# Weight remainders spread over 128 partitions, and V rows loaded from GpSimd's queue, in a two-layer recurrent-memory transformer kernel

## Chip, cores and metric

One core of one Trainium2 chip. The metric is the device time of one execution in microseconds; the kernel before takes 2640.42 us, the median of 3 runs (2637.03 to 2641.07).

## What is computed

Two identical layers on x of 2048 rows by 576 columns in bf16. A layer is attention over segments of 32 rows with a memory of 8 rows that the segment before left behind, then a gated feed-forward block of width 4608:

```python
for s in range(n_seg):                       # 64 segments of 32 rows
    h = concatenate([mem, x_segment])        # 8 + 32 rows
    q, k, v = h @ Wq, h @ Wk, h @ Wv         # 32 heads of 128
    p = softmax(mask(q @ k.T * scale))
    o = (p @ v) @ Wo
    mem = o[:8]; outs.append(o[8:])
x = x + attention(layernorm(x)); x = x + (silu(n @ w1) * (n @ w3)) @ w2   # n = layernorm(x)
# both lines once more, with the same weights
```

The memory makes the segments a chain: segment s needs the output of segment s - 1.

## The kernel before, in words

The 576 input columns are four chunks of 128 rows of the weights and a remainder of 64. `T.W` holds Wq in its parts 0 to 3, Wk in parts 4 to 7, and both remainders in part 8: Wq's on partitions 0 to 63, Wk's on 64 to 127, each 4096 columns wide. The remainder matmuls (`qk_tail`) use these two halves of TensorE's rows for q and k of one head at a time. `T.WV` holds Wv, with the 64-row remainder folded over both halves: blocks of 512 columns go alternately to partitions 0 to 63 and 64 to 127. `T.WO` holds Wo. All of it stays on chip.

The two layers run together, the second 8 segments behind the first, in 72 steps t. A step with both layers (t = 8 to 63) handles 32 heads in 4 groups g of 8: q and k, scores, softmax (VectorE and ScalarE), a DMA transpose of the probabilities from `PB` to `PTS` issued by SP, PV on TensorE, then Wo. `PB` has two buffers; after a transpose GpSimd clears the buffer (`pb_zero`, a memset), and VectorE then writes it for the next group but one. The feed-forward blocks run between the steps on TensorE, with w1, w3 and w2 streamed from HBM by SP.

At the start the rows of V that belong to the first layer's segments 9 to 16 are computed ahead ("VA"), since they depend on x alone, and stored to a DRAM tensor `XV`. In steps 9 to 16 each group loads its 32 rows by 1024 columns back into `T.V` (`va_load`, 64 KB, 32 loads), after the PV matmuls of the same group in the step before.

The order of the work comes from a planner (`plan`): each node has an engine, a cost and dependencies. TensorE's order is written out by hand as a string of letters (`ORDER`); for the other engines and queues ("DMA" is SP's, "SWD" GpSimd's, "ACT" ScalarE's) the planner takes the node that can start first by its costs. An engine then runs its instructions strictly in that order. `LOAD_BW` and the numbers in `node(...)` are such costs.

At the start SP issues, in this order: half of Wv's remainder, Wv in 8 loads of 512 KB, one load of x rows, the remainders of Wq and Wk, Wq and Wk in 16 loads, Wo in 4. ScalarE's queue issues two loads of 128 x rows, the 8 rows of mem0 and the other half of Wv's remainder. A completion semaphore is shared by every eighth hardware-queue load, and an issue waits for the load before it on its semaphore.

Lines that the prediction names: SP's loads are recorded on line 744 (`dma`), ScalarE's on 750 (`adma`), GpSimd's on 753 (`swdma`), transposes on 1290, the memset of `PB` on 1280, all matmuls on 735, ScalarE's work on 738 and VectorE's on 741. In the profile `W<-in_B_w_dram` is a feed-forward weight going to `W13`, since names are shown without their numbers.

Of the kernel before, what the change touches and what calls it, by code (L numbers as in the profile page):

```python
# [9 lines left out]
ACT = mybir.ActivationFunctionType  # L10
# [3 lines left out]
P = 128  # L14
R64 = 64
D = 576
NCH = D // R64
H = 32
E = 128
MEM = 8  # L20
SEG = 32
# [9 lines left out]
NV = 4  # L31
# [1 line left out]
R_HT = 6  # L33
PTR = 112
VAT = -9.5
LOAD_BW = {"ldqk": 400e3, "ldv": 410e3, "ldo": 360e3}
AH = (8, 17)
AROWS = (AH[0] + 1) * SEG
TRLAT = 2.5
# [29 lines left out]
def role(t):  # L69

    return (t - LAG) % 2


def pre(t):

    return AH[0] <= t <= AH[1]
# [194 lines left out]
def make_nodes(em, nseg, pools, o=Opt, dma_bw=230e3, load_bw=380e3, tail_bw=330e3):  # L271
# [4 lines left out]
    def node(*a, **k):  # L276
        n = Node(*a, **k)
        n.prio += 1e-9 * len(nodes)
        nodes.append(n)
        return n  # L280

    def banks(n=2):
        return [Slot("bank") for _ in range(n)]
# [12 lines left out]
    def load(name, nbytes, prio, fn, deps=()):  # L296
        return node("DMA", nbytes / LOAD_BW.get(name, load_bw), fn, deps=deps, prio=prio, name=name, lat=2.0)

    ld_m0 = node("ACT", 0.1, em.load_m0(), prio=-90, name="m0", lat=8.0)
    ld_t = [node("DMA", 1.3, em.load_vt(0), prio=-10.0, name="ldt", lat=2.0), node("ACT", 0.1, em.load_vt(1), prio=-80, name="ldt", lat=9.0)]  # L300
    ld_qt = node("DMA", 3.0, em.load_qt(), prio=-9.2, name="ldt", lat=2.0)
    ld_qk = [load("ldqk", kb(1024, H // 2 * E), i - 9.0, em.load_qk(i)) for i in (0, 1)]
    ld_h = [ld_qk[h0 // (H // 2)] for h0, _ in GROUPS]
    ld_v = [load("ldv", kb(512, 2048), VAT + 0.1 * i, em.load_v(i)) for i in (0, 1)]
# [3 lines left out]
    stored = []  # L308
    b = banks(1)
# [42 lines left out]
    vx_ev, last_v, pvs = {}, [], {}  # L352
# [46 lines left out]
    def step(t):  # L399
# [19 lines left out]
        for g, (h0, nh) in enumerate(GROUPS):  # L419
            qs, qe = [], []  # L420
            for uh, un in units(g, nl):
                q = Slot("qkt", users=1)
                b = banks()
                pq = t + o.qk + o.ustep * uh / 4
                m_ = node("PE", 8 * un * mmq, em.qk(t, uh, un, b), deps=hx + hm[:1] + ([ld_h[g]] if t == 0 else []),
                          prio=pq, mode="full", acq=[q] + b, name="QK")
                n = node("PE", un * mmq, em.qk_tail(t, uh, un, b), deps=hx + hm + ([ld_h[g], ld_qt] if t == 0 else []), prio=pq + o.qkt, mode="row",
                         acq=[q] + b, name="QKt")
# [18 lines left out]
            w = (1.04 - 0.07 * (e and not pre(t)) if nl == 2 else 0.46) * nh / 8  # L447
# [17 lines left out]
            b = banks(nl)  # L465
            ot = [Slot("ot") for _ in range(nl)]
            if pre(t) and t > AH[0]:
                kept = [d for blk in blks for d in vx_ev["VM", t - 1, blk]]
                if t < AH[1]:
                    kept.append(node("DMA", 0.3, em.va_load(t, g), deps=stored + [pvs[t - 1, g]], prio=t - 1 + o.gstep * g + 0.2, lat=2.4, ring=0.6, name="VAl"))  # L470
            else:
                kept = [d for blk in blks for d in vx_ev["VX", t - e, blk]]
            pv = node("PE", nh * mm80, em.pv(t, g, pts, b), deps=pe_ + kept + [d for blk in blks for d in vx_ev["VM", t, blk]],
                      prio=pf + o.pv, mode="full/col", acq=b + ot, rel=[pts], name="PV")
# [40 lines left out]
    kept = {}  # L515
# [165 lines left out]
    for t in range(nst):  # L681
        if t % 4 == 2 and (t + 2) // 4 < ngrp:
            x_in((t + 2) // 4)
        if t == LAG:
            ht_mem[t].append(node("DVE", 0.1, em.init_mem(1, LAG), deps=[m0e] + reads_ht.get(LAG - R_HT, []), prio=LAG - 2, name="m0"))
        if role(t) == 0 or t == 0:
            vx_pair(t - role(t), t - 1 + o.vx)
        step(t)
        if t == 0:
            opens = steps[0][f"WO{NG - 1}"]  # L690
            for nb, fn, es in stores:
                stored.append(node("DMA", 0.35 * nb, em.paced(fn, False, opens), deps=es + [opens], prio=0.5, lat=2.4, ring=0.35 * nb, name="VAs"))
        if t % 4 == 1 and t // 4 < ngrp:
            x_res(t // 4)
        if t % 4 == 3:
            job((t + 1) // 4 - 1)
        elif t == nst - 1:
            job(nst // 4)
# [12 lines left out]
class Emitter:  # L711
# [94 lines left out]
                    self.dma(self.T.W[:, 4 * kind + c, h], wd[c * P:(c + 1) * P, h])  # L806
        return f

    def load_vt(self, r):
        return lambda n: (self.adma if r else self.dma)(self.wv(True)[r * R64:(r + 1) * R64, :].rearrange("p (q n) -> p q n", q=NV),  # L810
                                                        self.a.wv[4 * P:D, :].rearrange("p (q r n) -> r p q n", q=NV, r=2)[r])

    def load_qt(self):
        def f(n):
            for r, wd in ((0, self.a.wq), (1, self.a.wk)):
                self.dma(self.T.W[r * R64:(r + 1) * R64, 8, :], wd[4 * P:D, :])
        return f

    def wv(self, tail):
# [304 lines left out]
    def va_load(self, t, g):  # L1124

        def f(n):
            r0, row = (t - AH[0] - 1) * SEG, 96 * role(t)
            self.dma(self.T.V[row:row + SEG, 2 * g:2 * g + 2, :], self.T.XV[r0:r0 + SEG, g * 1024:(g + 1) * 1024].rearrange("p (b n) -> p b n", n=512))
        return f

    def at(self, t):
# [32 lines left out]
    def qk_tail(self, t, uh, un, b):  # L1164
        def f(n):
            first = self.begin(b)
            for j in range(un):
                e0 = (uh + j) * E
                for kind in (0, 1):
                    rr = slice(kind * R64, (kind + 1) * R64)  # L1170
                    x, w = self.qk_rhs(t, rr, 4)
                    self.mm(self.bk(b[kind])[:, j * w:(j + 1) * w], self.T.W[rr, 8, e0:e0 + E], x,
                            first and j == 0, True, tile_position=(kind * R64, 0))
        return f

    def qk_ev(self, t, un, r, q, b):
# [328 lines left out]
def kernel(  # L1505
# [26 lines left out]
    em = Emitter(nc, tc, T, a, nseg)  # L1532
    pools = dict(POOLS)
    nodes = make_nodes(em, nseg, pools)

    wp = ctx.enter_context(tc.tile_pool(name="wts", bufs=1))
# [99 lines left out]
```

## Time and profile before

| | |
|---|---|
| median of 3 runs | 2640.42 us |
| profiled execution, its own time | 2643.07 us |
| its span, first to last instruction | 2641.3 us |
| mean granted TensorE clock | 0.994 |
| TensorE busy | 2563.1 us (97%) |
| VectorE, ScalarE, GpSimd busy | 2042.3, 1225.3, 338.1 us |
| moved by the DMA queues | 375.94 MB, mean 142 GB/s |
| V loads from XV | 32, issued between 269.0 and 526.1 us |

A row of a stretch gives its bounds, its length, the busy time of each engine with the count of its instructions, the granted clock of TensorE, the mean busy share of the 16 DMA engines, and what they moved. A row of the chain gives when a piece began, how long the chain stayed on it, and on what. A row of a DMA issue gives tensors, queue, count, size and the median time from issue to landing. In the timeline a bracket at a row's end tells the idle time before it and what ended it.

### The profile page before, as it was taken

How to read it: one execution, taken by the hardware profiler on the slowest of the kernel's cores; microseconds unless marked ns; L12 is line 12 of the kernel's file. 1: busy time of each engine (PE TensorE's matmuls, PEld its weight loads, DVE VectorE, ACT ScalarE, POOL GpSimd, SP SyncE). 2: the span in 40 equal slices, each digit the busy share in tenths (PEclk: the TensorE clock that was granted, in tenths of full speed). 3: DMA queues.
4: the chain of work that ended last, by engine and by line, in shares of the span. 5: the costliest groups of instructions: out<-in, count | busy, mean ns of one | idle time of the engine just before them, and what ended most of it. 6: DMA issues, size and time to landing. Idle time of an engine off the chain costs nothing.

```text
span 2641.3 us, 132672 instructions
## 1 busy us (share of the span) xinstructions
PE 2563.1 (97%) x58964; PEld 2182.5 (83%) x58991; DVE 2042.3 (77%) x5156; ACT 1225.3 (46%) x3492; POOL 338.1 (13%) x401
## 2 busy tenths in 40 slices
PE   6999999999999999999999999999999999999998
PEld 4788778888888888888888888888888888888887
DVE  5778777787888778778877877887787777788866
ACT  2545444544445354444535444453544445454543
POOL 1111111110111111111101101111111111011110
PEclk8999999999999999999999999999999999999999
DMA  9155747556555667555464655655575555554457
GB/s 308 56 154 139 183 106 179 143 134 155 129 135 115 151 127 155 134 132 138 110 144 126 158 137 126 146 112 139 120 166 134 135 135 112 135 121 141 127 156 239
DMA packets 690960, 375.94 MB, mean 142 GB/s; under 512 B 234728, under 2 KB 683248, under 8 KB 690128
## 3 DMA queue, kind: packets, MB, share of 16 engines
q1 hardware_dynamic: 686784, 359.94, 55.6%
q8 instruction: 461, 7.55, 1.2%
q0 software_dynamic: 3024, 6.93, 1.0%
q14 instruction: 115, 0.94, 0.1%
q10 hardware_dynamic: 576, 0.57, 0.1%
HBM read 309.11 MB, written 4.46 MB: 119 GB/s over the span
## 4 chain that ended last, share of the span: by engine, by line
PE 86%; DMA 7%; DVE 5%; issue 1%; ACT 1%; SPq 0%; POOL 0%; ACTq 0%; DVEq 0%; POOLq 0%
PE bank L735 86%; DMA PTS<-PB 2%; DMA W<-in_B_w_dram 1%; DMA W<-in_A_Wk_dram 1%; DVE STAT L741 1%; DMA W2C<-in_B_w_dram 1%; DVE SME L741 1%; DVE PB L741 1%; DVE V L741 1%; DVE HTT L741 1%; DMA WV<-in_A_Wv_dram 0%; ACT V L738 0%; SPq L744 0%; DVE QKT L741 0%; DVE XR L741 0%
## 5 line engine op out<-in xcount | busy, mean ns | idle before, releaser
L735 PEld LDWEIGHTS <-W 128*128 128x128 bf16 (+2 forms) x31776 | 1241.3, 100 | 131.8 <-issue 68.6
L735 PE MATMUL bank<-HT,W 128*128 128x80 bf16 (+2 forms) x23040 | 792.0, 197 | 16.6 <-issue 6.1
L735 PE MATMUL bank<-XTB,W 128*64 128x256 bf16 (+5 forms) x8736 | 661.4, 263 | 5.9 <-DMA W<-in_B_w_dram 3.1
L1280 POOL MEMSET PB<- 128x1024 bf16 x288 | 273.7, 951 | 1728.1 <-DMA PTS<-PB 950.9
L738 ACT ACTIVATE QKT<-bank 128x192 bf16<-128x192 f32 (+2 forms) x1505 | 356.0, 319 | 294.9 <-PE bank L735 286.0
L735 PE MATMUL bank<-OT,WO 128*128 128x80 bf16 (+3 forms) x11520 | 419.0, 198 | 5.7 <-issue 3.6
L735 PEld LDWEIGHTS <-WO 128*128 128x128 bf16 (+1 forms) x11520 | 386.4, 102 | 42.0 <-issue 30.0
L738 ACT ACTIVATE V<-bank 32x512 bf16<-32x512 f32 (+1 forms) x545 | 311.7, 586 | 164.7 <-PE bank L735 151.5
L735 PE MATMUL bank<-WV,HT 128*32 128x512 bf16 (+5 forms) x3777 | 347.7, 383 | 3.2 <-issue 2.5
L738 ACT ACTIVATE HTT<-bank 128x512 bf16<-128x512 f32 (+1 forms) x326 | 177.3, 549 | 312.6 <-PE bank L735 311.2
L735 PE MATMUL bank<-W2C,HTT 128*64 128x288 bf16 (+1 forms) x3224 | 314.8, 287 | 6.3 <-DMA W2C<-in_B_w_dram 2.9
L741 DVE TENSOR_REDUCE STAT<-SME 104x8 f32<-104x320 f32 (+1 forms) x576 | 274.7, 477 | 26.7 <-ACT SME L738 18.3
L741 DVE SCALAR_TENSOR_TENSOR XR<-bank,XR 128x288 f32<-128x288 f32 x574 | 242.1, 448 | 62.3 <-PE bank L735 57.6
L741 DVE TENSOR_TENSOR PB<-SME,STAT 40x128 bf16<-40x128 f32 (+4 forms) x932 | 276.6, 332 | 11.6 <-DVE STAT L741 0.4
L735 PEld LDWEIGHTS <-HTT 128*64 128x64 bf16 (+1 forms) x3304 | 226.5, 106 | 45.6 <-issue 8.7
L741 DVE SCALAR_TENSOR_TENSOR HTT<-HTT,bank 128x512 bf16<-128x512 bf16 (+1 forms) x324 | 200.8, 620 | 62.8 <-ACT HTT L738 59.7
L735 PEld LDWEIGHTS <-HT 128*32 128x32 bf16 (+5 forms) x3800 | 138.5, 101 | 128.5 <-issue 21.7
L738 ACT ACTIVATE OT<-bank 128x320 bf16<-128x320 f32 (+2 forms) x409 | 157.4, 399 | 172.6 <-PE bank L735 165.9
L741 DVE CAST V<-bank 64x512 bf16<-64x512 f32 (+1 forms) x287 | 196.6, 685 | 41.4 <-PE bank L735 35.4
L741 DVE TENSOR_TENSOR HTT<-HTT,bank 128x512 bf16<-128x512 bf16 (+1 forms) x324 | 203.6, 628 | 29.3 <-PE bank L735 0.9
L738 ACT ACTIVATE SME<-SME 104x320 f32<-104x320 f32 (+1 forms) x288 | 135.3, 470 | 173.3 <-DVE SME L741 171.7
L741 DVE CAST QKT<-bank 128x192 bf16<-128x192 f32 (+4 forms) x415 | 122.1, 335 | 89.7 <-PE bank L735 86.5
(64 smaller groups left out, 1413.5 us busy)
## 6 DMA issues: line engine op xcount, KB each, us to landing
W<-in_B_w_dram SPq DMA_DIRECT2D x608, 256.0 KB, 3.8
W2C<-in_B_w_dram SPq DMA_DIRECT2D x304, 288.0 KB, 3.9
W<-in_B_w_dram SPq DMA_DIRECT2D x608, 32.0 KB, 3.5
W<-in_B_w_dram SPq DMA_DIRECT2D x16, 512.0 KB, 6.9
W<-in_A_Wq_dram SPq DMA_DIRECT2D x9, 512.0 KB, 10.2
W<-in_A_Wk_dram SPq DMA_DIRECT2D x9, 512.0 KB, 10.2
WO<-in_A_Wo_dram SPq DMA_DIRECT2D x4, 1152.0 KB, 14.3
XR<-in_A_x_dram POOLq DMA_DIRECT2D x16, 288.0 KB, 3.1
```

The lines of the kernel that those rows point to most:

```text
L735: self.ch("PE", self.nc.tensor.matmul(out, lhsT=lhsT, rhs=rhs, start=start, stop=stop, skip_group_check=True, **k))
L738: self.ch("ACT", self.nc.scalar.activation(*a, **k))
L741: self.ch("DVE", getattr(self.nc.vector, fn_)(*a, **k))
L1280: return lambda n: self.ch("POOL", self.nc.gpsimd.memset(self.T.PB[:, pb.i, 0:GROUPS[g][1]], 0.0))
```

## The change

The remainders: Wv's is one load of 512 KB by SP into all 128 partitions (ScalarE's queue no longer takes part). Part 8 of `T.W` now holds, on partitions 0 to 63, Wq's heads 0 to 15 and Wk's heads 16 to 31, and on partitions 64 to 127 the other two. Wq's remainder is one load into 128 partitions of 2048 columns; Wk's is two loads of 64 rows by 2048 columns. `qk_tail` follows: for heads 16 to 31, q and k swap their halves. The 32 V loads go from SP's queue to GpSimd's. The planner's costs for these loads change; `ORDER` does not.

```diff
-LOAD_BW = {"ldqk": 400e3, "ldv": 410e3, "ldo": 360e3}
+LOAD_BW = {"ldqk": 405e3, "ldv": 405e3, "ldo": 357e3}
...
-    ld_t = [node("DMA", 1.3, em.load_vt(0), prio=-10.0, name="ldt", lat=2.0), node("ACT", 0.1, em.load_vt(1), prio=-80, name="ldt", lat=9.0)]
-    ld_qt = node("DMA", 3.0, em.load_qt(), prio=-9.2, name="ldt", lat=2.0)
+    ld_t = [node("DMA", 4.0, em.load_vt(), prio=-10.0, name="ldt", lat=2.0)]
+    ld_qt = node("DMA", 2.6, em.load_qt(), prio=-9.2, name="ldt", lat=2.0)
...
-                    kept.append(node("DMA", 0.3, em.va_load(t, g), deps=stored + [pvs[t - 1, g]], prio=t - 1 + o.gstep * g + 0.2, lat=2.4, ring=0.6, name="VAl"))
+                    kept.append(node("SWD", 1.0, em.va_load(t, g), deps=stored + [pvs[t - 1, g]], prio=t - 1 + o.gstep * g + 0.2, lat=4.0, name="VAl"))
...
-    def load_vt(self, r):
-        return lambda n: (self.adma if r else self.dma)(self.wv(True)[r * R64:(r + 1) * R64, :].rearrange("p (q n) -> p q n", q=NV),
-                                                        self.a.wv[4 * P:D, :].rearrange("p (q r n) -> r p q n", q=NV, r=2)[r])
+    def load_vt(self):
+        return lambda n: self.dma(self.wv(True).rearrange("p (q n) -> p q n", q=NV), self.a.wv[4 * P:D, :].rearrange("p (q r n) -> r p q n", q=NV, r=2))
 
     def load_qt(self):
         def f(n):
-            for r, wd in ((0, self.a.wq), (1, self.a.wk)):
-                self.dma(self.T.W[r * R64:(r + 1) * R64, 8, :], wd[4 * P:D, :])
+            w = H // 2 * E
+            self.dma(self.T.W[:, 8, 0:w], self.a.wq[4 * P:D, :].rearrange("p (r n) -> r p n", r=2))
+            for r in (1, 0):
+                self.dma(self.T.W[r * R64:(r + 1) * R64, 8, w:2 * w], self.a.wk[4 * P:D, (1 - r) * w:(2 - r) * w])
...
-            self.dma(self.T.V[row:row + SEG, 2 * g:2 * g + 2, :], self.T.XV[r0:r0 + SEG, g * 1024:(g + 1) * 1024].rearrange("p (b n) -> p b n", n=512))
+            self.swdma(self.T.V[row:row + SEG, 2 * g:2 * g + 2, :], self.T.XV[r0:r0 + SEG, g * 1024:(g + 1) * 1024].rearrange("p (b n) -> p b n", n=512))
...
             for j in range(un):
-                e0 = (uh + j) * E
+                up, hh = divmod(uh + j, H // 2)
                 for kind in (0, 1):
-                    rr = slice(kind * R64, (kind + 1) * R64)
+                    r0 = (kind ^ up) * R64
+                    rr, e0 = slice(r0, r0 + R64), (kind * H // 2 + hh) * E
                     x, w = self.qk_rhs(t, rr, 4)
                     self.mm(self.bk(b[kind])[:, j * w:(j + 1) * w], self.T.W[rr, 8, e0:e0 + E], x,
-                            first and j == 0, True, tile_position=(kind * R64, 0))
+                            first and j == 0, True, tile_position=(r0, 0))
```

SP's queue at the program's start, before (a row is line, operation, tile written and read, rows x columns, count):

```order
L744 DMA WV<-in_A_Wv_dram 64x4x512
L744 DMA WV<-in_A_Wv_dram 128x2048 x8
L744 DMA XN<-in_A_x_dram 128x576
L744 DMA W<-in_A_Wq_dram 64x4096
L744 DMA W<-in_A_Wk_dram 64x4096
L744 DMA W<-in_A_Wq_dram 128x2048 x4
```

and the same place after the change:

```order
L744 DMA WV<-in_A_Wv_dram 128x4x512
L744 DMA WV<-in_A_Wv_dram 128x2048 x8
L744 DMA XN<-in_A_x_dram 128x576
L744 DMA W<-in_A_Wq_dram 128x1x2048
L744 DMA W<-in_A_Wk_dram 64x2048 x2
L744 DMA W<-in_A_Wq_dram 128x2048 x4
```

Nothing moved past anything else; the first load doubled, Wq's remainder took 128 rows, and Wk's became two.

SP's queue where the first V loads stood, before (W_83 is the feed-forward tile W13):

```order
L1290 DMA_TRANSPOSE PTS<-PB 128x8x112
L744 DMA W_83<-in_B_w_dram 64x256 x2
L744 DMA V<-XV 32x1024 x2
L744 DMA W_83<-in_B_w_dram 64x256 x2
L1290 DMA_TRANSPOSE PTS<-PB 128x8x112
L744 DMA W_83<-in_B_w_dram 128x4x256 x2
L744 DMA V<-XV 32x1024
```

and after:

```order
L1292 DMA_TRANSPOSE PTS<-PB 128x8x112
L744 DMA W_83<-in_B_w_dram 64x256 x4
L1292 DMA_TRANSPOSE PTS<-PB 128x8x112
L744 DMA W_83<-in_B_w_dram 128x4x256 x4
L744 DMA W2C<-in_B_w_dram 128x2x576 x2
```

The V loads are gone from between the weight loads and transposes, whose own order is unchanged.

GpSimd's queue at the same steps, before (memsets of PB, reciprocal roots of the layer norms, an x load):

```order
L950 TENSOR_TENSOR LNS<-LNS,mhalf 128x1 x2
L1280 MEMSET PB 128x1024 x5
L753 DMA XR<-in_A_x_dram 128x576
L1280 MEMSET PB 128x1024
L950 TENSOR_TENSOR LNS<-LNS,mhalf 128x1
```

and after:

```order
L951 TENSOR_TENSOR LNS<-LNS,mhalf 128x1 x2
L1282 MEMSET PB 128x1024 x2
L753 DMA V<-XV 32x1024 x2
L1282 MEMSET PB 128x1024
L753 DMA V<-XV 32x1024
L1282 MEMSET PB 128x1024
L753 DMA V<-XV 32x1024
L1282 MEMSET PB 128x1024
L753 DMA XR<-in_A_x_dram 128x576
L1282 MEMSET PB 128x1024
L753 DMA V<-XV 32x1024 x2
```

A V load now stands between one clearing of a PB buffer and the next.

## The prediction

> **What bounds the kernel now.** I read the page's shares first, then the chain of work that ended last, then the first 60 us in stretches. The first lines below are the page's span and shares, the next its chain by engine, the rest pieces of the chain in order of time (start us, length us, what).
>
> ```profile
> span 2641.3 us, 132672 instructions
> PE 2563.1 (97%) x58964; PEld 2182.5 (83%) x58991; DVE 2042.3 (77%) x5156; ACT 1225.3 (46%) x3492; POOL 338.1 (13%) x401
> PE 86%; DMA 7%; DVE 5%; issue 1%; ACT 1%; SPq 0%; POOL 0%; ACTq 0%; DVEq 0%; POOLq 0%
> ```
>
> ```profile
> 2.32 10.56 DMA WV<-in_A_Wv_dram
> ...
> 14.28 13.22 DMA W<-in_A_Wk_dram
> 27.51 9.93 DMA W<-in_A_Wk_dram
> 37.46 10.20 DMA W<-in_A_Wk_dram
> 47.70 1.94 PE bank L735 x73
> ...
> 399.99 112.34 PE bank L735 x2519
> ```
>
> TensorE is the bound for nearly the whole span, but not at the start: up to 47.70 us the chain is a string of weight loads, first the Wv remainder on ScalarE's queue (2.32 to 12.88), then the Wk remainder (14.28 to 27.50), then the bulk of Wk. Whatever moves the last of these loads moves all that follows, because from there the chain runs on TensorE. So the loads at the start are worth their full length, and a load of step 9 to 16 only what it does to a wait of TensorE. The stretches of the start (columns: stretch, length, busy time of PE, PEld, DVE, ACT, POOL, granted clock, DMA share, GB/s):
>
> ```profile
> 2.00:12.00 10.00, 0.03 (x2) 0.03 (x3) 8.53 (x19) 1.28 (x1) 4.79 (x11) 1.00 0.99 288
> 12.00:18.00 6.00, 5.20 (x32) 2.45 (x34) 0.00 (x0) 0.70 (x1) 0.00 (x0) 1.00 1.09 399
> 18.00:28.00 10.00, 6.00 (x57) 2.67 (x53) 3.19 (x11) 2.43 (x7) 0.55 (x1) 0.84 0.98 231
> 28.00:38.00 10.00, 7.75 (x118) 3.45 (x118) 5.65 (x9) 5.30 (x9) 0.00 (x0) 0.99 1.03 409
> 38.00:48.00 10.00, 9.01 (x192) 6.34 (x190) 6.77 (x16) 2.40 (x5) 0.00 (x0) 0.83 1.04 401
> ```
>
> With 128-row loads alone the queues move 409 GB/s. In the two stretches that hold the 64-row remainders they move 288 and 231 at the same DMA share, so the DMA engines are occupied without moving bytes. What that costs: 10 x (1 - 288/409) = 3.0 us and 10 x (1 - 231/409) = 4.4 us, 7.3 us together (before rounding). This is what a better shape of these loads can win at most.
>
> **The remainders.** Bytes stay the same (512 KB for each of Wq, Wk, Wv); the shape changes, and with it, I think, the number of DMA engines that carry a load. The new source patterns of Wv and Wq have r, of size 2, as outermost dimension, over a destination of 128 rows. The trace has one load with an outermost count under 16, the 8 rows of mem0 on ScalarE's queue, q10. Below, the issues of that queue and its count of packets:
>
> ```profile
> XN<-in_A_x_dram ACTq DMA_DIRECT2D x2, 144.0 KB, 3.0
> WV<-in_A_Wv_dram ACTq DMA_DIRECT2D x1, 256.0 KB, 10.6
> XTB<-in_A_mem_dram ACTq DMA_DIRECT2D x1, 9.0 KB
> q10 hardware_dynamic: 576, 0.57, 0.1%
> ```
>
> Rows moved: 128 + 128 for XN, 8 for mem0, 64 x 4 for Wv, 520 in all. That leaves 56 packets of the 576, which fits one closing packet per DMA engine used: 16 + 16 + 16 and 8. The load of 8 rows ran on 8 engines. No row shows which pattern decides when source and destination differ (2 against 128), so both ends must be priced: two engines, or all 16.
>
> The Trainium skill's page "DMA: Bandwidth & Descriptors", section "Why a DMA increments its semaphore by 16 and not by 1", says that the engine count is the largest number up to 16 that divides the slowest dimension (not 1) of both patterns, which gives 2 here; the closing packets above agree with it for 8 and 16.
>
> Two engines: each then carries 256 KB of Wv and 256 KB of Wq. Dealt over 16, it would carry 32 KB of each. Extra: 448 KB, that is 458,752 bytes, on two engines, at 409/16 = 25.6 GB/s per engine: 17.9 us. Every other load of the start needs all 16 engines, so it ends when these two are through, and no later load catches up. The Wv rows are 1 KB packets. On q10, while it carries only the Wv remainder (7.4 to 12 us):
>
> ```profile
> q10 hardware_dynamic: 269, 0.26, 18.3%
> ```
>
> 18.3% of 16 x 4.6 us over 269 packets is 50 ns each, against 1024/25.6 = 40 ns at the full rate; 256 x 10 ns = 2.6 us at most. That row was measured beside another stream, so I take half, 1.3. What goes: the 7.3 us of the stretches above, since the two engines serve different halves of the partitions and the other 14 have long passed. Wk's remainder stays two 64-row loads, but by then the two late engines run alone. Sum: 17.9 + 1.3 - 7.3 = **+11.9 us**. Bounds of this case: +10.6 (no packet cost) to +20.5 (full packet cost, no stall goes away).
>
> Other edits there: the x rows on ScalarE's queue share the two engines and may land up to some 12 us later than their 3.0; the first use of Wv moves as far, so the loads cover it. ScalarE loses a DMA issue, takes the evictions of XTB and one QKT from VectorE and gives back one copy into W13: all under the wait for W, so nothing, and under 1 us without that cover. The matmuls of the remainder swap row halves for heads 16 to 31, same count and size: nothing. The granted clock is at half just after the loads (0.50 ahead of the last two columns):
>
> ```profile
> 60.00:62.00 2.00, 1.89 (x40) 1.24 (x37) 0.41 (x2) 0.83 (x2) 1.06 (x2) 0.50 0.07 17
> ```
>
> A longer idle start may lengthen or move such a stretch; I cost it at nothing, with 2 us on either side.
>
> **The V loads of steps 9 to 16.** 32 issues leave SP for GpSimd's queue (first row: shortest, median, longest ns; then pieces of SP's timeline; then what TensorE waited for between 230 and 560 us, as total, times, longest):
>
> ```profile
> L744 SPq DMA_DIRECT2D V<-XV x32: 303/452/1367, 269.0 to 526.1; - x32
> ```
>
> ```profile
> 337.26 0.45 SPq L744 DMA_DIRECT2D V<-XV  x1
> 339.02 1.22 SPq L1290 DMA_TRANSPOSE PTS<-PB  x1
> 340.29 1.10 SPq L744 DMA_DIRECT2D W2C<-in_B_w_dram  x2
> 341.49 3.18 SPq L744 DMA_DIRECT2D W<-in_B_w_dram  x4
> 344.77 1.24 SPq L1290 DMA_TRANSPOSE PTS<-PB  x1
> ...
> 374.28 1.88 SPq L744 DMA_DIRECT2D V<-XV  x2
> 376.33 1.35 SPq L1290 DMA_TRANSPOSE PTS<-PB  x1
> ```
>
> ```profile
> PE bank L735 <- DMA PTS<-PB: 5.4, 4, 2.2
> ```
>
> SP gets 32 x 0.452 = 14.5 us of issue time back, but TensorE waited only 5.4 us in all for transposes, and the one at 344.77 stands behind four weight loads (3.18 us), not behind a V load. Only at 374.28 does a pair of V loads (1.88 us) stand right ahead of a transpose. Gain: 0 to 1.9 us. On GpSimd each V load waits for the PV matmuls of the step before; behind it in its queue stands the memset that clears a PB buffer, for which VectorE's next write of that buffer and its transpose wait. Rows of GpSimd (an x load's issue, then two of those memsets):
>
> ```profile
> 300.14 0.57 POOL L753 DMA_DIRECT2D XR<-in_A_x_dram  x1
> ...
> 335.00 0.95 POOL L1280 MEMSET PB<- 128x1024 bf16 x1 [3.03 <-DMA PTS<-PB]
> 342.08 0.95 POOL L1280 MEMSET PB<- 128x1024 bf16 x1 [6.13 <-DMA PTS<-PB]
> ```
>
> The memset of 335.00 now stands behind the V load of 337.26. With 0.57 us for its issue it starts some 2.8 us late and ends near 338.8; two buffers alternate, and its buffer's next transpose is that of 344.77, so it is not late. Others are shifted by an issue or so. I cost the move at nothing, from -1.9 to +3 us (a late memset of this size that is waited for once).
>
> **Sum.** The profiled execution took 2643.07 us for its span of 2641.3; the median of the runs is 2640.42. 2643.07 + 11.9 + 0 = 2655.0, and 2.65 less for the median: about **2652 us**, 0.5% more than before. Own bounds of this case: 2640.4 + 10.6 - 1.9 - 2 = 2647 and 2640.4 + 20.5 + 3 + 2 = 2666; the upper end needs all at once, so I use 2662.
>
> **Rivals.**
>
> 1. *All 16 engines carry the new loads* (the destination's 128 rows decide). Then the change does what its shape suggests: the stalls go, except that Wk's remainder is still two 64-row loads. Half of the 4.4 us stays: -7.3 + 2.2 = -5.1 us, 2635; bounds -7.3 and -3.0 (the first stretch alone), so 2633 to 2637. For it: 288 and 231 GB/s against 409 with the 64-row shapes. Against it: 8 closing packets for 8 rows. It decides the sign: where more than about half of the extra bytes are spread over all 16 engines, the result is no longer slower. The Trainium skill's page named above, section "Rules for kernel authors", advises one 128-partition transfer in place of two to disjoint halves, which is this rival; the low GB/s beside the 64-row loads agrees with it.
> 2. *Two engines for each load, but not the same two.* Then each carries 224 KB extra: 9.0 + 1.3 - 7.3 = +3.0 us, 2643. Nothing in the trace tells engines apart.
> 3. *Two engines, and GpSimd's queue bites as well*: a V load held by its PV matmuls delays a memset that is waited for, 1 us in each of the 8 steps: 2652 + 8 = 2660. For it: the memset at 335.00. Against it: GpSimd is busy 13% of the span.
>
> **How the numbers follow.** Forecast 0.72, rival 1 0.18, rival 2 0.05, rival 3 0.05. A measurement of this kernel tells about 0.2% (5.3 us) from no change, so faster means under 2635.1 and slower over 2645.7. Rival 1 lies on the first border: half of it is faster, half the same. Rival 2 is the same, forecast and rival 3 are slower, less 0.01 for the forecast's low end: faster 0.09, same 0.15, slower 0.76. The forecast's own range, 2647 to 2662, holds with rival 3 about 0.70; to leave out no more than 2 in 10 the range must reach to the middle of rival 1: 2634 to 2662.
>
> **What would show it.** Right: the Wv remainder and the Wq remainder each land more than 10 us after their first byte, GB/s in the first 40 us is far under 409 while SP waits, the last Wk load lands near 59 instead of 47.7 us, and everything behind it is shifted by about 12 us and no more. The V loads then start some us earlier than on SP, and the wait for PTS stays near 5.4 us. Wrong: GB/s at 400 from 4 us on and the last Wk near 42 us (rival 1); or a shift that is right at 60 us and grows between 260 and 540 us (rival 3).

## The result, and the profile after

The changed kernel takes **2658.76 us** (median of 5 runs, 2653.08 to 2662.47) against 2640.42 (2637.03 to 2641.95) for the kernel before on the same chip: a ratio of 1.0069, 95% interval 1.0051 to 1.0088, or 18.3 us more (13.5 to 23.2). Single executions of one kernel scatter by 5 to 9 us, and here the profiled execution of after (2653.08) is the fastest of its five, while that of before (2643.07) is slower than all five of before's. So the cost is taken from the medians, and the two traces are compared at places near the start, not at their ends. Other chips run the kernel before at 2632 to 2637 us; below, each version is given as a ratio to the runs of before on its own chip. In two versions below one execution had a much lower granted clock (0.753 and 0.881), and the ratios leave it out.

Span, shares, and the chain by engine, of after:

```profile
span 2651.3 us, 132692 instructions
PE 2560.9 (97%) x58964; PEld 2182.4 (82%) x58991; DVE 2042.6 (77%) x5155; ACT 1226.4 (46%) x3493; POOL 354.2 (13%) x433
PE 84%; DVE 6%; DMA 6%; issue 1%; ACT 1%; SPq 1%; POOL 0%; DVEq 0%; POOLq 0%; ACTq 0%
```

TensorE's busy time is the same to 0.1% (2560.9 against 2563.1 us): no work was added, it starts later. Where, the chain up to the first matmuls on the whole of Wk tells (start, length, what):

```profile
1.53 8.16 SPq L744
...
10.21 10.02 DMA WV<-in_A_Wv_dram
20.23 0.02 issue
20.25 3.41 SPq L744
23.66 0.04 issue
23.71 20.30 DMA W<-in_A_Wk_dram
...
44.03 10.22 DMA W<-in_A_Wk_dram
54.25 0.02 issue
54.27 10.23 DMA W<-in_A_Wk_dram
64.50 0.05 issue
64.54 1.94 PE bank L735 x73
```

The piece of 73 matmuls that began at 47.70 us now begins at 64.54, **16.8 us later**. Ahead of it stand the same loads, one Wk load of 20.30 us among them (the second half of Wk's remainder). The spans of the two traces lie only 10.0 us apart: between 175 and 417 us the shift of the same matmuls goes from 15.1 to 9.0. The traced execution of before falls behind there against every version below, by 5.6 to 9.7 us whatever that version changes, so this belongs to that execution and not to the change. The same stretches of the start as before (busy time of PE, PEld, DVE, ACT, POOL; clock; DMA share; GB/s):

```profile
2.00:12.00 10.00, 0.03 (x2) 0.03 (x2) 8.53 (x19) 1.28 (x1) 4.81 (x11) 1.00 0.34 100
12.00:18.00 6.00, 1.00 (x12) 0.79 (x14) 0.00 (x0) 0.70 (x1) 0.00 (x0) 1.00 0.98 318
18.00:28.00 10.00, 6.74 (x51) 3.06 (x47) 1.87 (x6) 1.94 (x6) 0.00 (x0) 1.00 0.88 294
28.00:38.00 10.00, 6.40 (x43) 2.72 (x44) 2.30 (x6) 1.30 (x2) 0.55 (x1) 0.66 0.89 242
38.00:48.00 10.00, 4.95 (x77) 1.93 (x75) 5.49 (x8) 4.71 (x8) 0.00 (x0) 0.92 0.51 166
48.00:58.00 10.00, 4.14 (x89) 3.19 (x91) 0.69 (x1) 1.21 (x3) 0.00 (x0) 0.50 1.01 380
```

Two stretches have idle DMA engines (shares 0.34 and 0.51), and from 12 to 38 us they are busy but move 242 to 318 GB/s. A closer cut shows how many engines work in the idle parts:

```profile
6.00:9.00 3.00, 0.00 (x0) 0.00 (x0) 2.78 (x7) 0.03 (x1) 0.00 (x0) 1.00 0.14 49
38.50:42.00 3.50, 3.50 (x72) 1.51 (x64) 1.30 (x2) 1.43 (x3) 0.00 (x0) 1.00 0.13 53
28.00:36.00 8.00, 4.56 (x28) 1.90 (x28) 1.61 (x5) 0.70 (x1) 0.55 (x1) 0.58 0.92 240
```

A share of 0.13 to 0.14 of 16 engines is 2.1 to 2.2 engines: first the Wv remainder alone, then the Wq remainder alone. The completion semaphores say the same. A load raises its semaphore by 16 in all. Those of the Wv and the Wq load move once early (at 1.85 and 19.93 us) and then only twice more (last at 16.61 and 42.12 us): 14 increments at once, two late ones. These two loads, then, run on **two engines**. The loads behind them show the wait: of the first whole Wq load behind the remainders, 14 increments come between 29.10 and 30.61 us and the other two at 44.14 and 44.96. The Trainium skill, page "DMA: Bandwidth & Descriptors", section "Why a DMA increments its semaphore by 16 and not by 1", takes the count of engines from the outer dimensions of both patterns, which gives 2; the 0.13 here agrees.

The V loads on GpSimd's queue, and TensorE's wait for transposes from 230 to 560 us:

```profile
V<-XV POOLq DMA_DIRECT2D x32, 64.0 KB, 3.9
PE bank L735 <- DMA PTS<-PB: 3.3, 2, 2.0
```

The wait went from 5.4 to 3.3 us (the last column is the longest single one): nothing that could carry 18 us either way.

### The profile page after: what moved, and what is told of

The parts are those of the page before. It is cut to its first block, busy times and chain, and to the rows that moved or that the text cites. A ratio compares the mean times of both kernels' runs of the same rounds, so it can differ in the third digit from the quotient of the medians.

```text
span 2651.3 us, 132692 instructions
## 1 busy us (share of the span) xinstructions
PE 2560.9 (97%) x58964; PEld 2182.4 (82%) x58991; DVE 2042.6 (77%) x5155; ACT 1226.4 (46%) x3493; POOL 354.2 (13%) x433
## 4 chain that ended last, share of the span: by engine, by line
PE 84%; DVE 6%; DMA 6%; issue 1%; ACT 1%; SPq 1%; POOL 0%; DVEq 0%; POOLq 0%; ACTq 0%
PE bank L735 84%; DMA PTS<-PB 2%; DMA W<-in_A_Wk_dram 2%; DVE STAT L741 1%; DMA W<-in_B_w_dram 1%; DVE PB L741 1%; DVE SME L741 1%; DMA W2C<-in_B_w_dram 1%; DVE HTT L741 1%; DVE V L741 1%; SPq L744 1%; DMA WV<-in_A_Wv_dram 0%; DVE XR L741 0%; DVE QKT L741 0%; ACT V L738 0%
## 5 line engine op out<-in xcount | busy, mean ns | idle before, releaser
L738 ACT ACTIVATE QKT<-bank 128x64 bf16<-128x64 f32 (+2 forms) x1506 | 356.3, 319 | 305.5 <-PE bank L735 296.9
L741 DVE CAST QKT<-bank 128x128 bf16<-128x128 f32 (+4 forms) x414 | 121.6, 335 | 89.6 <-PE bank L735 86.5
```

Of the source, the lines that this page charges most:

```text
L738: self.ch("ACT", self.nc.scalar.activation(*a, **k))
L741: self.ch("DVE", getattr(self.nc.vector, fn_)(*a, **k))
```

## The experiments

A folded load, below, is the Wv or Wq remainder as one load of 128 rows whose source pattern has r, of size 2, outermost. Theory at the outset: the folded loads run on the same two engines, all loads at the start wait for these two, and the V loads play no part. Rivals: GpSimd's queue; the new layout of the remainders; different engines for each load; and, later, what makes the shift 16.8 instead of 11.9 us.

### The two parts of the change apart

Only the remainders (V loads, and their nodes in the planner, back on SP):

```diff
-            self.swdma(self.T.V[row:row + SEG, ...
+            self.dma(self.T.V[row:row + SEG, ...
```

> The remainders of the change alone; the 32 V loads stay on SP. Theory (two engines carry the Wv and the Wq remainder): as slow as the whole change, 2652 to 2662 us, last Wk load landing near 64 us. Rival (the V loads on GpSimd's queue are what costs): back near the kernel before, 2637 to 2644.

Measured: 2650.36 us, ratio 1.0078 (1.0057 to 1.0098), last Wk load landed at 64.77 us. And only the V loads, with their nodes, on top of the kernel before:

```diff
-            self.dma(self.T.V[row:row + SEG, ...
+            self.swdma(self.T.V[row:row + SEG, ...
```

> The kernel before with the 32 V loads alone moved to GpSimd. Theory: the same as before within 3 us, 2637 to 2643. Rival (GpSimd's queue holds memsets that are waited for): 2648 or more.

Measured: 2631.43 us, ratio 0.9996 (0.9982 to 1.0009). The whole cost is in the remainders; GpSimd's queue (rival 3) falls.

### The shape of the source pattern alone

The changed kernel with Wv's and Wq's remainders each as two loads of 64 rows; layout, matmuls and order as in the change (shown for Wq; Wv's in the same way):

```diff
+            for r in (0, 1):
+                self.dma(self.T.W[r * R64:(r + 1) * R64, 8, 0:w], self.a.wq[4 * P:D, r * w:(r + 1) * w])
-            self.dma(self.T.W[:, 8, 0:w], self.a.wq[4 * P:D, :].rearrange("p (r n) -> r p n", r=2))
```

> The whole change, but the Wv and the Wq remainder are each issued by SP as two loads of 64 rows, so that no pattern's outermost count is under 64; same bytes into the same places. Theory: the last Wk load lands near 48 us again and the time is 2637 to 2644. Rival (the new layout, the doubled first load on SP or the new order costs, not the count of engines): stays at 2652 or more.

Measured: 2634.62 us, ratio 1.0007 (0.9993 to 1.002). Its stretches from 18 us on, and its chain at the last Wk load:

```profile
18.00:28.00 10.00, 6.20 (x59) 2.69 (x55) 3.39 (x11) 2.64 (x7) 0.55 (x1) 0.85 1.04 287
28.00:38.00 10.00, 8.79 (x171) 4.48 (x170) 5.69 (x9) 5.72 (x11) 0.00 (x0) 0.98 1.02 408
```

```profile
35.27 10.21 DMA W<-in_A_Wk_dram
45.48 0.04 issue
45.53 1.94 PE bank L735 x73
```

The same bytes into the same places, with an outermost count of 64 in place of 2, and the last Wk load lands at 45.5 instead of 64.5 us. The loss is gone, and the layout is not its cause.

From here on this is the version in pieces. From it, one folded load at a time. First Wq's:

> As the kernel with 64-row pieces, but the Wq remainder is again the one load of 128 rows with an outermost source count of 2; Wv's stays in two pieces. Theory (each such load adds its own lag, since both use the same two engines): about half of the whole change's cost, 6 to 10 us over the kernel with pieces, last Wk load near 56 us. Rival (the two loads use different engines, or only the longer one counts): all of the cost, or none of it.

Measured: 2643.65 us, ratio 1.005 (1.0032 to 1.0069). Its stretch 28 to 38, a piece of it, and its chain:

```profile
28.00:38.00 10.00, 6.64 (x90) 2.55 (x89) 5.64 (x9) 5.30 (x9) 0.00 (x0) 0.97 0.47 156
```

```profile
31.00:35.00 4.00, 3.61 (x68) 1.37 (x60) 2.04 (x3) 2.16 (x4) 0.00 (x0) 1.00 0.13 52
```

```profile
46.51 10.32 DMA W<-in_A_Wk_dram
56.84 0.05 issue
56.88 1.94 PE bank L735 x73
```

Then Wv's alone:

> The changed kernel with Wq's remainder as two loads of 64 rows and Wv's remainder as the one load in the pattern (r p q n): the mirror image of the run that kept only Wq's load in that pattern (2643.65 us, +9.0 over the version in pieces, 2634.62). Two engines: this half of the pair costs as much by itself, about 6.7 to 9 us over the version in pieces, 2641 to 2644, the last Wk load near 55 us, and the semaphore of the Wv load gets two late increments. Rival (the cost sits where SP's issues are held up behind the Wq load, and the Wv load is covered because TensorE needs Wv only bit by bit): 2635 to 2637, last Wk near 46 to 47.

Measured: 2651.29 us, ratio 1.006 (1.0046 to 1.0075), last Wk at 55.99. At the loads both are as expected: 56.84 and 55.99 against 45.48, +11.4 and +10.5 us. The time of the second came out above its 2641 to 2644; on its chip the kernel before is 3.2 us slower, which leaves some 4 us, and the intervals of the two ratios overlap. Both folded loads together end 19.0 us later than the version in pieces, a little less than the 21.9 of the two sums. So the costs add, and the two loads use the same engines: rival 2, whose second load would have cost nothing, falls. The semaphores of the changed kernel agree: behind both loads it is two increments of a 128-row load that lag, not four.

### Why 16.8 and not 11.9 us

My first idea was the 64-row loads of Wk that are left: they would slow the two engines. The changed kernel with Wk's remainder as one load of 128 rows (other rows of Wk, so that this part of k is not the reference's):

```diff
-            for r in (1, 0):
-                self.dma(self.T.W[r * R64:(r + 1) * R64, 8, w:2 * w], ...)
+            self.dma(self.T.W[:, 8, w:2 * w], self.a.wk[0:P, 0:w])
```

> The changed kernel with Wk's remainder as one load of 512 KB into 128 partitions, from rows 0 to 127 of Wk instead of rows 512 to 575 (so the remainder's part of k is left out and another is computed). Theory: the stall of 64-row loads did not go away; it slows the two engines' 4 KB packets from about 160 to 250 ns while the Wk halves run. Without 64-row loads the Wq remainder lands near 39 instead of 42 us, 28 to 38 us moves over 300 GB/s instead of 242, the last Wk load lands 3 to 4 us earlier (near 61), and the time falls by as much, 2655 against 2658.8. Rival (the excess over 11.9 us is SP's held-up issues alone): last Wk at 64 to 65, no change within 1 us.

Measured: 2653.96 us, ratio 1.0073 (1.0056 to 1.009).

```profile
28.00:38.00 10.00, 8.87 (x92) 3.78 (x96) 1.27 (x3) 1.57 (x3) 0.55 (x1) 0.83 0.94 254
```

```profile
52.88 10.25 DMA W<-in_A_Wk_dram
63.12 0.05 issue
63.17 1.94 PE bank L735 x73
```

The last Wk load lands 1.4 us earlier (63.12 against 64.50), of the 4.9 us to be explained, and the ratio did not fall. With no 64-row load left the stretch still moves 254 GB/s at a share of 0.94. The theory falls: what is slow there goes with the folded load running beside whole ones, by a mechanism that this run does not show. The rival as I had put it (SP's held-up issues alone) is not shown by that either.

Next, the packets of the folded Wv load, 4 KB instead of 1 KB (the columns then lie in another order than the matmuls read, so this part of v is not the reference's):

```diff
-        ... self.a.wv[4 * P:D, :].rearrange("p (q r n) -> r p q n", q=NV, r=2))
+        ... self.a.wv[4 * P:D, :].rearrange("p (r n) -> r p n", r=2))
```

> The changed kernel with Wv's remainder still one load on two engines, but in rows of 4 KB instead of 1 KB (the columns of Wv's remainder then lie in another order than the matmuls read, so the remainder's part of v is another one). It sets the packet term apart. In the changed kernel the load ran from 1.85 to 16.61 us, with 1 KB packets of 46 ns alone and 70 ns beside the bulk of Wv. Theory: 64 packets of 4 KB at 160 ns take 10.2 us beside the x rows' 1 us, so it lands near 13.5 to 14.5, everything behind it on the two engines comes 2 to 3 us earlier, the last Wk load lands near 62 instead of 64.5, and the time is 2 to 3 us under the 2658.8 of the changed kernel (ratio to before near 1.006). Rival (the two engines lose their time to the streams beside them, not to packet size): it still lands near 16, last Wk at 64 to 65.

Measured: 2655.49 us, ratio 1.0068 (1.0055 to 1.0082); the Wv remainder landed at 16.52 us (16.61 with 1 KB), the last Wk load at 64.63 (64.50). As the rival said, it lands no earlier. That does not show that packet size costs nothing, since a second thing changed, the issue behind it, in the chain:

```profile
1.52 0.41 SPq L744
1.93 0.04 issue
1.97 0.43 SPq L744
2.40 0.04 issue
2.45 17.82 DMA WV<-in_A_Wv_dram
```

With 1 KB packets the next issue took 8.16 us, so apart from the x rows the two engines had the Wv remainder to themselves up to then; with 4 KB packets it takes 0.41, and the bulk of Wv runs beside it at once. The packets alone can be read in the changed kernel: from 6 to 9 us, with the load alone, a 1 KB packet takes 46 ns, against 40 at 25.6 GB/s, which is an estimated 256 x 6 ns = 1.5 us. So the likely reading, not tested apart, is that the earlier bulk of Wv took back what larger packets gained.

### What a fast start is worth

What if all three remainders were loads of 128 consecutive rows, on 16 engines? The version in pieces with such loads, from other rows of the weights (the remainders' values are left out):

```diff
+        return lambda n: self.dma(self.wv(True), self.a.wv[0:P, 0:NV * 512])
...
+            self.dma(self.T.W[:, 8, 0:w], self.a.wq[0:P, 0:w])
+            self.dma(self.T.W[:, 8, w:2 * w], self.a.wk[0:P, 0:w])
```

> The version in pieces (2634.62 us) with all three remainders as one natural load of 128 rows by 4 KB on 16 engines, from other rows of the weights (so the remainders' values are left out). It is the floor that the change could reach: no 64-row load, no 1 KB packet, no folded source. If the 64-row shapes cost the 7.3 us that the prediction put on them, the first 40 us move 400 GB/s throughout, the last Wk load lands near 41 to 42 us against 45.5 and 47.7, and the time is 3 to 5 us under the version in pieces, 2630 to 2632, about 0.2% under the kernel before. Rival (the low stretches are the start of the stream and x rows, not the shapes): last Wk at 45, time as in pieces.

Measured: 2638.35 us, ratio 1.0013 (1.0002 to 1.0024), though the last Wk load landed at 41.38 us, 6.3 us ahead of the kernel before. The same loads in the kernel before, with its layout and order, all on SP's queue:

> The kernel before with its remainders as natural loads of 128 rows by 4 KB from other rows of the weights (the remainders' values are left out), all on SP's queue; layout, order of all engines and V loads as before. It asks what faster loads at the start are worth at all. In the version with 128-row loads on top of the change the last Wk load landed at 41.4 us, 4.1 us ahead of the version in pieces, and TensorE was not a microsecond earlier at 100 us, since its chain then ran over the V rows computed ahead and ScalarE's evictions of them. If that floor is the kernel's own: last Wk near 41 to 42 us (before 47.7), the 1000th matmul at most 3.5 us earlier than before, and the time 0 to 3.5 us under before (ratio 0.9987 to 1.0). Rival (the floor belongs to the changed layout and order, which cost something of their own): all 6 us arrive, ratio near 0.9977.

Measured: 2629.96 us, ratio **0.9978** (0.9968 to 0.9987), 6.1 us less for a last Wk load that landed at 41.56, 6.1 us earlier. So the floor that I had read into TensorE's own work is not the kernel's; the rival is right. What TensorE waited for from 18 to 40 us, first in the version on top of the change, then in the kernel before with these loads:

```profile
PE bank L735 <- DVE XN L741: 3.8, 1, 3.8
```

```profile
PE bank L735 <- DVE XN L741: 0.5, 1, 0.5
```

and VectorE's statistics of the third 128 x rows, in the same order:

```profile
22.38 0.81 DVE L741 BATCH_NORM_STATS2 LNS<-XN 128x6 f32<-128x288 bf16 x2
```

```profile
17.30 0.82 DVE L741 BATCH_NORM_STATS2 LNS<-XN 128x6 f32<-128x288 bf16 x2 [5.38 <-DMA XN<-in_A_x_dram]
```

In the changed order they stand behind three copies of YTS and two casts of W13, which wait for TensorE; in the order of before they come first and wait for nothing but the rows. The kernel before waits 4.0 us at this place too, but there the rows land only at 21.85 us; with 128-row loads they are there at about 17.2, and the order decides. I took the planner's new numbers for the reason of the changed order. To test that, only those numbers back, on top of the former of the two (remainders' values left out again):

```diff
-LOAD_BW = {"ldqk": 405e3, "ldv": 405e3, "ldo": 357e3}
+LOAD_BW = {"ldqk": 400e3, "ldv": 410e3, "ldo": 360e3}
-    ld_t = [node("DMA", 4.0, ...
+    ld_t = [node("DMA", 1.3, ...
-    ld_qt = node("DMA", 2.6, ...
+    ld_qt = node("DMA", 3.0, ...
```

> The version with 128-row loads on top of the change (remainders' values left out; 1.0013 of before, although its last Wk load landed at 41.4 us), with one edit: the planner's numbers for these loads as before (LOAD_BW, 1.3 and 3.0). TensorE's and VectorE's order is then that of before, row for row; layout of the remainders, the loads themselves and V rows on GpSimd's queue stay changed. Theory: those numbers moved VectorE's statistics of the third 128 x rows behind the copies of YTS and two casts of W13 (22.38 us instead of 17.30), TensorE waited for the transposes of those rows until 25, and that ate what the loads gained. Then the statistics start near 17.3 us again, TensorE's transposes of them near 21.4, and the ratio is that of the same loads in the kernel before, 0.9978 (0.997 to 0.9987). Rival (the layout, with q and k swapping halves, or V rows on GpSimd's queue costs it): 1.001 again.

Measured: 2636.02 us, ratio 0.9993 (0.9981 to 1.0005).

```profile
17.23 0.82 DVE L741 BATCH_NORM_STATS2 LNS<-XN 128x6 f32<-128x288 bf16 x2 [5.30 <-DMA XN<-in_A_x_dram]
```

```profile
30.84 10.24 DMA W<-in_A_Wk_dram
41.08 0.05 issue
41.12 1.94 PE bank L735 x73
```

At the start it is as expected: the statistics at 17.23, and the chain again ends on the last Wk load. Of the time 0.20% came back, short of the 0.9978 that I expected; the interval overlaps that of the kernel before with these loads (on another chip) by a little only. Whether layout or V loads keep the last 0.15% is not settled.

The same numbers with the loads in 64-row pieces, the whole computation again, as the version that might beat both kernels:

> The whole computation again: the version in 64-row pieces (2634.62 us, 1.0007 of before on its chip, last Wk at 45.5 us) with the planner's numbers of before and so the order of before on TensorE and VectorE. It is the version of this change that could beat both kernels: loads that end 2.2 us earlier than before, and no changed order to take it back. Theory: last Wk near 45.5, TensorE 2 us earlier than before from there, ratio 0.9985 to 1.0 (2 us is under what a measurement of this kernel tells from no change). Rival (order plays no part): 1.0007 again.

Measured: 2637.34 us, ratio 1.0002 (0.9991 to 1.0014), last Wk at 45.40. It beats the changed kernel and is not to be told from the one before. Both what I expected (0.9985 to 1.0) and the rival's 1.0007 reach into its interval, so this run does not show what the order is worth in this version.

Last, could two 64-row loads into opposite halves run side by side at the full rate? The version in pieces with the lower halves on SP's queue and the upper ones on ScalarE's, all ahead of the bulk of Wv (shown for Wq; Wv's and Wk's in the same way):

```diff
-                self.dma(self.T.W[r * R64:(r + 1) * R64, 8, 0:w], ...
+                (self.adma if r else self.dma)(self.T.W[r * R64:(r + 1) * R64, 8, 0:w], ...
-    ld_qt = node("DMA", 2.6, em.load_qt(), prio=-9.2, name="ldt", lat=2.0)
+    ld_qt = node("DMA", 2.6, em.load_qt(), prio=-9.9, name="ldt", lat=2.0)
```

> The version in pieces with the lower 64-row halves of all three remainders on SP's queue and the upper ones on ScalarE's, all six issued at the start, ahead of the bulk of Wv. If a 64-row load is slow because all engines write the same half of the partitions, then two such loads for opposite halves side by side run near 400 GB/s: the 1.5 MB take about 4 us, the last Wk load lands near 42 to 43 us, and the time is 2 to 4 us under the version in pieces, 2631 to 2633. Rival (a 64-row load is slow by itself, whatever runs beside it): 2 to 12 us stay near 290 GB/s, the last Wk near 45 to 46, time as in pieces or, since Wv's bulk starts some 4 us later, 1 to 3 us above it.

Measured: 2639.93 us, ratio 1.0015 (1.0005 to 1.0025).

```profile
2.00:12.00 10.00, 0.00 (x0) 0.00 (x0) 8.19 (x18) 1.28 (x1) 4.52 (x11) 1.00 0.98 228
```

228 GB/s at a share of 0.98. The first microseconds of the stretch are slow even with no 64-row load in it (269 GB/s from 2 to 7 us in the kernel before with 128-row loads), so the fair comparison is 7 to 12 us here, 217 GB/s, with 20 to 25 us in the version in pieces, where one half follows the other: 235. Side by side is no better, and the rival is right in this; the last Wk load landed at 44.24 us, later than the 42 to 43 of the theory and 1.2 us before the version in pieces, a gain that the time does not show.

## Why the prediction was right, and where its sum was not

- **Two engines** for the folded loads: right. DMA shares of 0.13 and 0.14 where such a load runs alone, and ratios of 1.005 and 1.006 for either load by itself against 1.0007 for the pieces.
- **17.9 us of extra bytes at 25.6 GB/s per engine**: the rate is right where the two engines run alone (53 GB/s at a share of 0.13, 2.08 engines, is 25.5 each).
- **The packet term, +1.3**: right in size where the Wv load runs alone (46 ns a packet against 40, 1.5 us in all). At the last load nothing is to be seen of it (64.50 with 1 KB, 64.63 with 4 KB packets), but that run changed the issue behind the load as well.
- **The stalls that go, -7.3**: this step failed, and it is the largest error of the sum. I said that the two engines serve different halves and "the other 14 have long passed", so that the loss at the 64-row loads would vanish. The two engines do not run alone for most of the time: from 28 to 36 us the engines are busy to 0.92 and move 240 GB/s, 240 / (16 x 0.92) = 16.3 GB/s per busy engine against 24.8 before with whole loads (409 at 1.03). One slow pattern was exchanged for another. By what was measured at the last Wk load, 16.8 - 17.9 = -1.1 us came back, or -2.4 if the packet term is counted, not -7.3. (This takes the 17.9 as whole and books all slowness beside other loads here; why the engines are slow beside a folded load stays open, and no run shows which engine writes which half.) That puts the start at +16.8 in place of +11.9, and the whole at +18.3 (13.5 to 23.2), in which 16.8 lies; the 1.5 us beyond it are within the scatter. The range that I gave for the case, 2647 to 2662, held because its upper bound let no stall go; the middle, 2652, lies 6.8 us under the 2658.76 measured.
- **A last Wk load near 59 us, and a shift of about 12 us and no more**: wrong by the same step; it landed at 64.5, and the shift is 16.8.
- **The V loads at nothing**: right (0.9996), with the wait for transposes at 3.3 us in the changed kernel.
- **The other edits "under the wait for W, so nothing, and under 1 us without that cover"**: the first half is right, the second wrong. In the changed kernel the reordered statistics wait for their x rows anyway:

```profile
28.98 0.82 DVE L741 BATCH_NORM_STATS2 LNS<-XN 128x6 f32<-128x288 bf16 x2 [2.16 <-DMA XN<-in_A_x_dram]
```

  Without that cover the same order makes TensorE wait 3.8 us once (128-row loads on top of the change), and seems to cost about 0.2% (1.0013 against 0.9993, on two chips, with intervals that just overlap). I had counted which copies changed engines, not in which order VectorE then does them.
- **Rival 1** (all 16 engines, 2635) was wrong in its premise, and its price would not have been paid out in full either: even with no 64-row load at all the changed order gives 1.0013. The same loads in the order of before gain 6.1 us, so the 7.3 us that I read from 288 and 231 GB/s were somewhat too many. The excess is in the first stretch: from 2 to 12 us that version moves only 335 GB/s, though no 64-row load is in it, so some 1.8 of the 3.0 us booked there are not the shapes. The Trainium skill's page "DMA: Bandwidth & Descriptors", section "Rules for kernel authors", prefers one transfer to 128 partitions over two to disjoint halves; with this source pattern, which leaves the one transfer on two engines, the measurement says otherwise (1.0069 against 1.0007), and it decides.

## What to carry to other kernels

Before a load is folded over the partitions, look at the outermost count of both patterns and at the DMA share while the load runs: a big load that keeps two engines busy delays every later load that needs all sixteen. A term "what is slow now will go" needs the rate of what takes its place. And when costs in a planner change, compare the order of every engine near the stretch that the change is to shorten, since a gain there is only as large as the next wait allows.

## What the runs showed of the hardware that was not expected

- Behind a load that gives each of two engines 256 packets of 1 KB, the next DMA issue on the same queue took 8.16 us (7.99 to 8.29 in three other versions with this load); behind the same bytes in 64 packets of 4 KB, 0.41 us in one.
- Beside the folded Wq load, all engines are slow: 240 to 254 GB/s at shares of 0.92 and 0.94, also where no load of 64 rows is left; without folded loads and 64-row loads it is 409 at 1.03. Why was not settled; collisions of the two engines' writes with those of the others were not tested.
- Two 64-row loads into opposite halves of the partitions from two queues, side by side: 217 GB/s from 7 to 12 us, against 235 from 20 to 25 us where one such load follows the other on one queue.
